# Two halves for the last output tile of a sliding-window attention and token-mixing kernel, with all instruction orders solved anew

## The chip, the cores and the metric

The kernel runs on one core of a Trainium2 chip. The metric is the device time of one execution in microseconds; the median of three runs is 137.68 us (136.97 to 139.27). The engines are PE (matrix products and transposes), ACT (activations and copies), DVE (elementwise work and copies), POOL (here mostly the issuing of loads and some stores) and SP (which only issues stores and two first loads).

## What is computed

The inputs are q, k and v of 8 batches, 8 heads, 576 positions and 64 elements per head, and three weights. For each batch and head there is attention over a causal window of 128 positions with a linear bias by distance; the heads are put side by side to a row x of 512, and a token mixer follows:

```
scores = q @ k.T / 8 - slope[h] * |distance|     where 0 <= distance < 128
attn   = exp(scores - max) / sum
x      = concat over heads of attn @ v           # 576 x 512 per batch
W      = (x @ w_q) @ (x @ w_k).T / 8             # 576 x 576 per batch
out    = relu(W @ x) @ w_out                     # 576 x 512 per batch, float32
```

The kernel uses that W @ x is (x @ w_q) @ ((x @ w_k).T @ x), so that W is never made.

## The kernel before, in words

The kernel is a list of some 775 operations with names, each put on one engine. A text, ORDER, names them one by one with their engine (P, A, V, G for POOL, S for SP), the PSUM bank of a matmul operation, and a number of filling matmuls ahead of it. The loop at line 885 walks this text and emits each operation; every engine then works through its own in that order, one after the other, and waits where the data of its next operation is not ready. The order comes from a planner outside the kernel, which uses the costs written beside each operation (for instance `pe(0.865, 0.2)`). In the names, the first number is the batch.

- L (Lq, Lk, Lv, Lt, Lw..): loads, all issued by POOL, except FQ0 and FQ1, the two halves of the first q tile, which SP issues and CQ0, CQ1 turn into 16 bits. `load` (line 366) lets each load wait for an earlier one, so that only a few are in flight.
- TW, TN, TT: transposes of q and k on PE, and ETW, ETN, ETT their evictions. QK: scores of a group of blocks. EXP: the exponential of 128 x 1024 scores on ACT (line 610), 64 in all. MUL: the product with the bias (line 617, DVE). PV: the product with v. X: normalization (lines 655 and 656, DVE).
- XT, WQ, WK, G, MX with their evictions EXT, EWQ, EWK, EG, RM: the token mixer of a batch.
- OUT (`add_out`, line 800): an output tile of 128 positions by 512 columns, four matmuls that are summed in one bank; EO: its eviction into a free buffer on ACT or DVE; DO: its store from SP or POOL. Tiles whose number ends in 4 hold the last 64 positions of two batches, and take two DMAs.
- At the start stand constants: iota (POOL), idh, perm, dist and mask (DVE), bias0 and bias1 (ACT), and memsets (ones0 to ones4, zeros, zerop, pads), which can be put on DVE or POOL.
- HOLD: from its place in the order on, the next store of SP also waits for one of the last loads (`gate`, lines 224 to 227).

The last tile, OUT7.3, is special: its one bank is evicted in two halves of 256 columns (HO7.3.0 on ACT, HO7.3.1 on DVE) into the buffer osb_end, with two stores (DO7.3.0 on SP, DO7.3.1 on POOL). Both evictions name the whole operation OUT7.3 as what they wait for.

`apart` (line 243) tells the scheduler which instructions need not wait for each other: those on different engines that use different halves of a pair of PSUM banks, and those of one named group, which write different columns of one buffer.

Of the kernel before, what the change touches and what calls it, by code (L numbers as in the profile page):

```python
# [45 lines left out]
QK0.3.1:P:0:1 ETW1.1.1:A PV0.0:P:3 Lv0.4:G MUL0.2.1:V EXP0.3.1:A PV0.1:P:2 X0.0:V Lk2.1:G  # L46
QK1.0.1:P:1 QK1.1.1:P:0 EXP1.0.1:A Lq2.1:G X0.1:V PV0.2:P:3 EXP1.1.1:A MUL0.3.1:V XT0.0:P:2
QK0.3.0:P:1 Lk2.0:G X0.2:V EXP0.3.0:A QK1.3.1:P:0 MUL1.0.1:V QK1.2.1:P:3 Lq2.0:G EXP1.2.1:A
TW1.0:P:1 MUL0.3.0:V MUL1.1.1:V Lv1.0:G EXT0.0:A PV0.3:P:3 ETW1.0.0:V ETW1.0.1:A Lwk:G
PV0.4:P:2 EXP1.3.1:A X0.3:V Lv1.1:G QK1.1.0:P:1 wqq:V EXP1.1.0:A QK1.0.0:P:3 QK1.2.0:P:0  # L50
Lv1.2:G X0.4:V EXP1.0.0:A XT0.1:P:1 Lv1.3:G MUL1.3.1:V TW2.1:P:2 EXP1.2.0:A MUL1.2.1:V
Lv1.4:G WQ0.0:P:30 EXT0.1:V ETW2.1.0:A Lt1.0:G XT0.2:P:31 QK1.3.0:P:0 ETW2.1.1:A EWQ0.0:V
WQ0.1:P:10 MUL1.1.0:V EXT0.2:A EXP1.3.0:A QK2.0.1:P:2 Lwo.3:G MUL1.0.0:V WQ0.2:P:11
TW2.0:P:3 EXP2.0.1:A EWQ0.1:V Lwo.2:G MUL1.3.0:V Lk3.0:G PV1.0:P:0 ETW2.0.1:A MUL1.2.0:V
WK0:P:10 ETW2.0.0:A X1.0:V Lt1.1:G PV1.1:P:2 EWQ0.2:A EWK0:A QK2.0.0:P:3 X1.1:V Lwo.1:G
PV1.2:P:1 EXP2.0.0:A QK2.2.1:P:0 Lq3.0:G X1.2:V PV1.3:P:2 EXP2.2.1:A PV1.4:P:3 Lt1.3:G
X1.3:V XT1.0:P:1 QK2.1.0:P:0 Lt1.2:G EXT1.0:A X1.4:V G0:P:20 EXP2.1.0:A Lwo.0:G XT1.1:P:1
Lv2.3:G EG0:V XT1.2:P:21 WQ1.0:P:30 EXT1.1:A MUL2.0.1:V EXT1.2:A MX0.0:P:0 EWQ1.0:A Lk3.1:G
MX0.1:P:1 MX0.2:P:2 RM0.2:V WQ1.2:P:31 WK1:P:30 RM0.1:A Lq3.1:G RM0.3:V RM0.4:A WQ1.1:P:01
EWK1:A Lv2.0:G RM0.0:V QK2.1.1:P:2 EWQ1.1:A QK2.2.0:P:1 EXP2.1.1:A MUL2.1.0:V G1:P:30  # L60
Lv2.2:G EWQ1.2:V TW3.0:P:0 EXP2.2.0:A EG1:V MUL2.1.1:V Lq4.1:G MX1.1:P:2 ETW3.0.0:A TT1:P:3
ETW3.0.1:V MX1.0:P:1 Lv2.1:G RM1.3:A OUT0.2:P:00 RM1.1:V RM1.2:A Lv2.4:G MUL2.2.1:V RM1.0:A
OUT1.3:P:01 ETT2:A ETT3:V Lk4.0:G EO0.2:A MUL2.2.0:V QK2.3.0:P:1 QK2.3.1:P:2 EO1.3:V Lk4.3:G
EXP2.3.0:A QK3.0.0:P:3 OUT1.2:P:00 MUL2.0.0:V EXP2.3.1:A Lq5.2:G MUL2.3.0:V TW3.1:P:1
EO1.2:V Lv3.1:G EXP3.0.0:A PV2.0:P:2 MUL2.3.1:V OUT0.0:P:01 Lk4.1:G ETW3.1.1:A X2.0:V
ETW3.1.0:A PV2.3:P:3 Lk4.2:G EO0.0:A QK3.0.1:P:1 X2.3:V PV2.1:P:2 Lq4.0:G EXP3.0.1:A
QK3.1.0:P:0 QK3.1.1:P:3 X2.1:V Lv3.0:G EXP3.1.0:A OUT1.1:P:10 MUL3.0.0:V Lt2.3:G EXP3.1.1:A
PV2.2:P:2 MUL3.1.0:V PV2.4:P:0 Lq4.3:G EO1.1:A X2.2:V QK3.3.1:P:3 Lq4.2:G OUT0.1:P:11
EXP3.3.1:A X2.4:V Lv3.2:G XT2.1:P:2 MUL3.1.1:V MX1.2:P:3 EO0.1:A QK3.2.0:P:0 OUT0.3:P:10
Lt2.2:G RM1.4:A EXT2.1:V EXP3.2.0:A MUL3.0.1:V Lv3.3:G XT2.2:P:11 XT2.0:P:3 QK3.3.0:P:2  # L70
EXT2.2:A EO0.3:V TN4.1.0:P:0 Lk5.1:G EXP3.3.0:A OUT1.4:P:11 ETN4.1.0:V Lv4.0:G MUL3.2.0:V
EXT2.0:A QK3.2.1:P:0 TN4.1.1:P:2 MUL3.3.1:V EXP3.2.1:A TN4.0.0:P:3 Lt2.0:G OUT1.0:P:10
ETN4.1.1:V Lt2.1:G ETN4.0.0:A MUL3.3.0:V TN4.0.1:P:0 EO1.4:A Lk5.0:G QK4.0.1:P:2 ETN4.0.1:V
PV3.0:P:3 EXP4.0.1:A WQ2.0:P:11 MUL3.2.1:V Lq5.1:G PV3.1:P:0 EWQ2.0:A X3.0:V QK4.1.1:P:2
EO1.0:A Lv3.4:G WK2:P:11 EXP4.1.1:A X3.1:V Lq5.0:G WQ2.1:P:10 EWK2:A QK4.1.0:P:3 MUL4.0.1:V
XT3.0:P:2 Lq5.3:G EXP4.1.0:A QK4.0.0:P:0 EXT3.0:V G2:P:11 Lv4.1:G EWQ2.1:V EXP4.0.0:A
PV3.2:P:2 MUL4.1.0:V Lk5.2:G QK4.2.1:P:3 EG2:A X3.2:V PV3.3:P:0 EXP4.2.1:A Lv4.2:G TT2:P:1
X3.3:V MX2.1:P:2 ETT5:A MX2.0:P:3 Lk6.2:G RM2.1:A WQ3.0:P:11 RM2.3:V ETT4:A PV3.4:P:0
EWQ3.0:A Lk5.3:G RM2.0:V RM2.2:A QK4.2.0:P:2 TN5.1.0:P:1 X3.4:V EXP4.2.0:A OUT2.3:P:30
Lv4.4:G MUL4.0.0:V Lv4.3:G ETN5.1.0:A QK4.3.0:P:0 TN5.0.1:P:2 MUL4.1.1:V EO2.3:A TN5.0.0:P:1  # L80
# [853 lines left out]
```

## Time and profile before

| | |
|---|---|
| median of three runs | 137.68 us (136.97 to 139.27) |
| the profiled execution | 136.75 us |
| its span, first to last instruction | 134.9 us |
| granted TensorE clock, mean | 0.990 |
| first exponential starts | 9.70 us |
| last exponential starts | 110.89 us |
| last matmul ends | 129.78 us |
| last store is issued, and lands | 130.94 us, 2.0 us later |

All times in the profile count from the start of the span. A row of the timeline gives the start, the duration, the engine, the line of the kernel, the operation, what it writes and reads with its shape, how many instructions are merged in the row and, in brackets, how long the engine sat idle before it and what ended that wait. Rows of neighbours overlap a little, since the end of one instruction and the start of the next are pipelined. A row of a group gives the busy sum, the mean in ns and the idle time ahead of it. Most matmuls have the line of the helper `mm` (L216), transposes L219, evictions L231 to L239, loads L222 and stores L225.

### The profile page before, as it was taken

Reading aid. Unit: us, or ns where it says so; the run is one execution under the profiler, and the core shown is the slowest. Engines: PE = TensorE matmul, PEld = TensorE weight load, DVE = VectorE, ACT = ScalarE, POOL = GpSimd, SP = SyncE. Lnnn points to the kernel's source line nnn. Section 1 sums busy time; section 2 is a strip of 40 time slices with the busy share of each in tenths; the row PEclk is TensorE's granted clock in tenths of the full one; section 3 lists DMA queues with packets and bytes.
Section 4 is the critical chain, followed back from the end, with each engine's and each line's share of the span. In section 5 each row is a group of like instructions: output and inputs, shape, how many; then the busy total and the mean of one; then the engine's idle time right before and its main releaser. Section 6 shows DMA issues by size and latency. Waiting matters only on the chain.

```text
span 134.9 us, 5631 instructions
## 1 busy us (share of the span) xinstructions
PE 124.2 (92%) x2390; PEld 82.8 (61%) x2390; DVE 112.4 (83%) x252; ACT 115.6 (86%) x191; POOL 100.0 (74%) x149
## 2 busy tenths in 40 slices
...
GB/s 117 153 183 172 168 179 195 183 152 163 165 178 173 156 155 156 154 154 145 148 150 139 144 149 140 145 140 150 313 217 256 381 305 84 311 174 237 301 313 69
DMA packets 92855, 24.86 MB, mean 184 GB/s; under 512 B 80256, under 2 KB 89344, under 8 KB 92832
## 3 DMA queue, kind: packets, MB, share of 16 engines
...
q14 instruction: 5, 0.04, 0.1%
...
## 4 chain that ended last, share of the span: by engine, by line
POOL 52%; DMA 19%; PE 15%; issue 10%; POOLq 0%; ACT 0%
POOL natw L222 24%; POOL vt L222 16%; PE pair L216 14%; DMA natw<-in_k_dram 11%; DMA vt<-in_v_dram 8%; POOL natt L222 6%; POOL out_dram L225 4%; POOL wout_sb L222 2%; PE pair L219 1%; ACT natw L231 0%; POOLq L929 0%; POOL wk_sb L222 0%; POOL wint L289 0%; POOLq L222 0%; ACT wqT L231 0%
## 5 line engine op out<-in xcount | busy, mean ns | idle before, releaser
L610 ACT ACTIVATE pt<-pair 128x1024 f16<-128x1024 f32 x64 | 63.5, 1038 | 2.7 <-PE pair L216 1.7
L222 POOL DMA_DIRECT2D vt<-in_v_dram x40 | 37.9, 1019 | 2.2 <-DMA vt<-in_v_dram 0.8
L617 DVE TENSOR_TENSOR pt<-pt,bias 128x1024 f16<-128x1024 f16 x48 | 32.1, 682 | 0.1
L216 PE MATMUL pair<-wout_sb,rm 128*128 128x512 f16 x128 | 32.0, 380 | 0.0
L225 POOL DMA_DIRECT2D out_dram<-natw x17 | 10.4, 709 | 19.2 <-ACT natw L231 19.2
L222 POOL DMA_DIRECT2D natw<-in_k_dram x24 | 23.0, 1000 | 1.6 <-DMA natw<-in_q_dram 1.4
L216 PEld LDWEIGHTS <-pt 128*128 128x128 f16 x576 | 20.5, 97 | 5.8 <-issue 3.2
L216 PE MATMUL pair<-qkT 64*128 64x256 f16 (+3 forms) x352 | 22.9, 243 | 1.2 <-ACT pt L610 0.5
L216 PE MATMUL pair<-vt,pt 128*128 128x65 f16 x576 | 23.4, 193 | 0.6 <-DMA vt<-in_v_dram 0.4
L656 DVE TENSOR_TENSOR x<-pair,inv 128x512 f16<-128x512 f32 x32 | 22.1, 692 | 1.1
L222 POOL DMA_DIRECT2D natw<-in_q_dram x23 | 21.9, 1017 | 0.6 <-DMA natw<-in_k_dram 0.4
L216 PEld LDWEIGHTS <-rm 128*128 128x128 f16 x128 | 10.6, 97 | 11.2 <-issue 1.3
L216 PEld LDWEIGHTS <-qkT 64*128 64x128 f16 x352 | 11.2, 94 | 7.5 <-issue 3.7
L219 PEld LDWEIGHTS <-natw 128*64 128x64 f16 (+1 forms) x512 | 12.8, 102 | 4.6 <-issue 2.4
L231 ACT COPY natw<-pair 128x512 f32<-128x512 f32 x21 | 12.7, 612 | 1.7 <-PE pair L216 1.7
L756 ACT ACTIVATE rm<-pair 128x512 f16<-128x512 f32 x20 | 11.3, 613 | 1.6 <-PE pair L216 1.5
L617 DVE TENSOR_TENSOR pt<-pt,biasl 128x1024 f16<-128x1024 f16 x16 | 10.9, 683 | 0.2 <-ACT pt L610 0.2
L219 PE MATMUL pair<-permh,natw 128*64 128x128 f16 x256 | 8.8, 220 | 1.5 <-ACT pt L610 1.2
L655 DVE RECIPROCAL inv<-pair 128x8 f32<-128x8 f32 (+1 forms) x40 | 8.1, 203 | 2.2 <-PE pair L216 2.0
L216 PE MATMUL pair<-xT,wqq_sb 128*128 128x256 f16 x64 | 9.5, 274 | 0.0
L216 PE MATMUL pair<-fill 128*128 128x512 f16 x22 | 7.7, 504 | 1.6 <-DVE fill L347 1.2
L498 ACT COPY qkT<-pair 128x512 f32<-128x512 f32 x12 | 7.0, 625 | 1.5 <-PE pair L219 1.5
...
## 6 DMA issues: line engine op xcount, KB each, us to landing
vt<-in_v_dram POOLq DMA_DIRECT2D x32, 128.0 KB, 5.9
...
natw<-in_q_dram POOLq DMA_DIRECT2D x16, 128.0 KB, 5.2
natw<-in_k_dram POOLq DMA_DIRECT2D x16, 128.0 KB, 5.1
...
```

What stands on the lines that cost most here:

```text
L216: hold(nc.tensor.matmul(*a, **k))
L219: hold(nc.tensor.transpose(*a))
L222: hold(nc.gpsimd.dma_start(**k))
L225: i = (nc.gpsimd if eng == "POOL" else nc.sync).dma_start(**k)
L231: hold(nc.scalar.copy(out_ap, in_ap))
L498: hold(nc.scalar.copy(dst, src))
L610: nc.scalar.activation(out=pt[:, 0:1024], in_=two(s.bank).rearrange("p e c -> p (e c)"), func=AF.Exp, scale=SCALE)
L617: nc.vector.tensor_tensor(out=pt[:, 0:1024], in0=pt[:, 0:1024], in1=bt, op=ALU.mult)
L655: nc.vector.reciprocal(out=inv[r], in_=pxv[r, :, :, 64])
L656: nc.vector.tensor_tensor(out=x[r].rearrange("p (g h d) -> p g h d", g=2, h=4), in0=pxv[r, :, :, 0:64], in1=inv[r].unsqueeze(3).broadcast_ ...
L756: hold(nc.scalar.activation(out=out_ap, in_=in_ap, func=AF.Relu, scale=WSCALE))
```

## The change

The last tile becomes two operations, OUT7.3.1 and OUT7.3.0, of four matmuls on 256 columns each, in two PSUM banks of different pairs. Each has its own eviction and store; the two evictions are put in a group (`last`), since they write different columns of osb_end. HO7.3.1 goes to ACT and its store to SP; HO7.3.0 goes to DVE and its store to POOL.

The whole ORDER is solved anew by the planner, so nearly every operation changes its place, and some their engine or bank: the set of names is the same but for OUT7.3. Filling matmuls are 31 in place of 22, zerop goes from POOL to DVE and zeros from DVE to POOL, stores are shared differently by SP and POOL, and HOLD stands at the end, behind all stores. The diff, with those lines of ORDER that start and end it or bear on the stores:

```diff
 ORDER = """
-FQ1:S ones0:V FQ0:S iota:G Lk0.0:G ones3:V ones1:V Lk0.1:G idh:V zeros:V Lq0.1:G CQ1:A
-dist:V Lk1.1:G CQ0:A mask:V Lt0.3:G Lt0.1:G perm:V bias0:A pads:V Lq1.1:G TW0.0.0:P:00:13
-Lt0.2:G ones4:V TW0.0.1:P:01 ETW0.0.0:V Lt0.0:G ETW0.0.1:A zerop:G bias1:A QK0.2.0:P:1:3
-QK0.1.0:P:2 Lv0.0:G EXP0.1.0:A TW0.1:P:0:5 Lv0.1:G EXP0.2.0:A QK0.0.0:P:3 ETW0.1.1:A
-ETW0.1.0:V Lv0.2:G EXP0.0.0:A biasl1:V QK0.2.1:P:0 QK0.1.1:P:1 MUL0.2.0:V QK0.0.1:P:2
-Lq1.0:G EXP0.1.1:A biasl0:V Lk1.0:G EXP0.0.1:A MUL0.0.0:V TW1.1:P:1 ones2:G MUL0.1.1:V
-EXP0.2.1:A MUL0.0.1:V TT0:P:2 Lv0.3:G ETW1.1.0:A ETT0:V MUL0.1.0:V Lwq:G ETT1:A
...
-OUT4.0:P:11 EXP6.3.0:A PV6.0:P:0 DO1.1:G OUT4.3:P:10 X6.0:V EXP6.1.1:A Lv7.4:G TN7.0.0:P:3
...
-EXP6.3.1:A X5.4:V OUT4.1:P:30 DO3.2:G MUL6.1.1:V ETN7.1.0:A XT5.2:P:31 QK6.1.0:P:0 XT5.1:P:2
...
-PV6.4:P:0 Lv7.3:G MUL6.2.0:V WQ5.2:P:30 DO3.3:S WQ5.1:P:31 ETN7.1.1:A PV6.1:P:2 X6.4:V
...
-EXT6.0:A G5:P:20 DO1.0:S EXP7.2.1:A MUL7.0.0:V HOLD:S DO4.1:S MX4.2:P:3 XT6.1:P:0 EG5:V
...
-EWQ6.1:V QK7.3.1:P:0 EWK6:A MUL7.1.1:V MX5.1:P:3 EXP7.3.0:A G6:P:21 MUL7.0.1:V OUT5.1:P:20
-RM5.1:A MUL7.3.0:V EXP7.3.1:A MUL7.2.1:V OUT5.0:P:10 RM5.3:A EG6:V PV7.1:P:0 MUL7.3.1:V
-EO5.1:A OUT5.3:P:11 EO5.0:A DO5.1:S X7.1:V DO5.0:G MX6.0:P:3 MUL7.2.0:V MX6.1:P:2 EO5.3:A
-DO2.0:G PV7.4:P:0 RM6.3:A DO5.3:S PV7.3:P:1 RM6.0:A X7.4:V OUT5.2:P:21 DO4.2:S RM6.2:A
-X7.3:V RM6.1:A PV7.0:P:0 PV7.2:P:3 EO5.2:A X7.0:V OUT6.3:P:20 X7.2:V OUT6.1:P:10 EO6.3:A
-MX5.2:P:0 XT7.2:P:11 DO6.3:G XT7.0:P:3 EO6.1:V EXT7.2:A XT7.1:P:2 EXT7.0:A OUT6.0:P:11
-DO4.0:G EXT7.1:V RM5.4:A DO6.1:G WQ6.2:P:10 WK7:P:00 EWQ6.2:A EO6.0:A WQ7.2:P:30 WQ7.1:P:01
-EWQ7.2:V EWK7:A DO6.0:G WQ7.0:P:31 EWQ7.1:A G7:P:30 DO3.4:G EWQ7.0:A MX6.2:P:2 OUT5.4:P:10
-EG7:A RM6.4:V DO2.3:G MX7.0:P:0 DO5.2:G MX7.1:P:3 EO5.4:V MX7.2:P:2 OUT6.2:P:11 RM7.1:A
-RM7.4:V DO5.4:S RM7.2:V RM7.0:A OUT7.4:P:10 RM7.3:A EO6.2:V OUT7.1:P:00 DO6.2:S EO7.4:A
-OUT7.2:P:01 DO7.4:S EO7.1:V OUT7.0:P:20 DO7.1:G EO7.2:A OUT7.3:P:21 DO7.2:S EO7.0:A DO7.0:S
-HO7.3.0:A HO7.3.1:V DO7.3.0:S DO7.3.1:G
+FQ0:S ones3:V FQ1:S Lk0.0:G zerop:V iota:G ones2:V Lk0.1:G pads:V Lq0.1:G dist:V Lt0.2:G
+CQ1:A idh:V mask:V Lq1.1:G zeros:G perm:V bias1:A Lk1.1:G TW0.0.1:P:00:13 CQ0:A Lt0.0:G
+bias0:A ETW0.0.1:V TW0.0.0:P:01:1 Lt0.3:G ones0:V ones4:G ones1:V ETW0.0.0:A biasl0:V
+QK0.1.0:P:1:5 Lv0.0:G QK0.0.0:P:2 biasl1:V EXP0.1.0:A QK0.2.0:P:3 Lt0.1:G TW0.1:P:0:1
+EXP0.0.0:A Lv0.1:G ETW0.1.1:V ETW0.1.0:A Lv0.2:G EXP0.2.0:A MUL0.0.0:V QK0.1.1:P:1:4
+QK0.2.1:P:2 MUL0.1.0:V Lk1.0:G QK0.0.1:P:0 EXP0.2.1:A MUL0.2.0:V Lq1.0:G TW1.1:P:3:2
+EXP0.0.1:A MUL0.2.1:V Lv0.3:G EXP0.1.1:A MUL0.0.1:V Lv0.4:G ETW1.1.0:V ETW1.1.1:A TT0:P:0:4
+Lq2.0:G MUL0.1.1:V PV0.0:P:2 ETT1:A QK1.0.1:P:1 ETT0:V Lk2.0:G X0.0:V EXP1.0.1:A QK0.3.0:P:0
...
+EO1.4:A Lt2.1:G ETN4.0.0:V XT2.1:P:3 EXP3.2.0:A OUT1.0:P:01 DO1.2:G MUL3.3.0:V EXT2.1:A
...
+OUT2.0:P:11 Lv5.2:G EXP5.0.0:A MUL5.0.1:V XT4.1:P:0 Lq6.3:G QK5.2.1:P:3 EO2.0:A MUL5.0.0:V
+QK5.2.0:P:2 EXP5.2.1:A OUT3.1:P:10 DO2.0:S EXT4.1:V Lt3.3:G MUL5.1.1:V EXP5.2.0:A
...
+OUT4.0:P:11 EXP6.1.1:A X6.0:V PV5.4:P:0 EO4.1:V EO4.0:A QK6.3.1:P:2 TN7.1.1:P:3 X5.4:V
+EXP6.3.1:A DO4.0:S OUT4.2:P:11 DO2.2:S MUL6.1.1:V ETN7.1.1:A XT5.2:P:10 TN7.0.0:P:0 DO3.4:S
+TN7.1.0:P:2 EO4.2:V EXT5.2:A QK6.3.0:P:3 ETN7.1.0:A OUT3.3:P:10 MUL6.2.0:V DO4.2:G
+EXP6.3.0:A DO0.3:S MUL6.3.1:V WQ5.0:P:11 DO4.1:G DO0.1:S ETN7.0.0:A EO3.3:V TN7.0.1:P:2
+DO3.1:G XT5.1:P:3 EWQ5.0:A ETN7.0.1:V QK6.2.1:P:0 EXT5.1:A PV6.1:P:1 Lv7.1:G MUL6.3.0:V
+EXP6.2.1:A WQ4.2:P:20 QK7.1.0:P:3 X6.1:V DO3.0:G WK5:P:21 EWQ4.2:A EXP7.1.0:A PV6.4:P:0
+DO1.4:G MUL6.2.1:V WQ5.2:P:20 EWK5:A QK7.1.1:P:1 X6.4:V EWQ5.2:A PV6.2:P:3 EXP7.1.1:A
+DO2.3:G QK7.0.1:P:2 X6.2:V PV6.3:P:0 DO1.1:G EXP7.0.1:A WQ5.1:P:10 MUL7.1.0:V Lv7.4:G
+XT6.0:P:3 EWQ5.1:A QK7.0.0:P:2 X6.3:V Lv7.0:G EXT6.0:A XT6.2:P:11 G5:P:10 EXP7.0.0:A
+EXT6.2:V MX4.2:P:3 Lv7.2:G XT6.1:P:0 EG5:V WQ6.0:P:11 RM4.4:A EXT6.1:V MX5.0:P:2 MUL7.0.1:V
+QK7.3.1:P:3 MX5.1:P:0 RM5.0:A WK6:P:10 MUL7.1.1:V RM5.2:A WQ6.1:P:20 EWQ6.0:V EXP7.3.1:A
+EWK6:V OUT5.0:P:21 RM5.3:V RM5.1:A MUL7.3.1:V QK7.3.0:P:1 EWQ6.1:A QK7.2.0:P:3 EXP7.3.0:A
+QK7.2.1:P:0 EO5.0:V G6:P:20 MUL7.0.0:V EXP7.2.1:A OUT5.3:P:21 EG6:V MUL7.3.0:V EXP7.2.0:A
+MX6.0:P:1 MX6.1:P:0 MUL7.2.1:V OUT5.1:P:20 EO5.3:A RM6.0:V RM6.2:A DO5.3:G PV7.4:P:3
+MUL7.2.0:V RM6.3:A PV7.0:P:1 DO2.1:G OUT6.0:P:21 RM6.1:A X7.4:V EO5.1:A DO5.0:G PV7.1:P:0
+X7.0:V EO6.0:A PV7.3:P:3 DO0.0:G X7.1:V OUT6.3:P:20 DO6.0:S DO1.3:S X7.3:V PV7.2:P:1 EO6.3:A
+DO3.3:S WQ6.2:P:21 OUT5.2:P:00 X7.2:V DO6.3:G XT7.2:P:01 XT7.0:P:3 EWQ6.2:V DO0.2:G EO5.2:A
+EXT7.2:V XT7.1:P:1 MX5.2:P:2 OUT6.1:P:01 EXT7.0:A EXT7.1:V DO4.3:G RM5.4:V WK7:P:00 EO6.1:A
+WQ7.2:P:30 WQ7.0:P:31 EWK7:V DO6.1:S WQ7.1:P:10 EWQ7.0:V DO5.2:S MX6.2:P:2 EWQ7.1:A G7:P:00
+RM6.4:A DO5.1:S OUT5.4:P:11 EG7:A DO3.2:S EWQ7.2:A MX7.2:P:0 DO1.0:S MX7.0:P:2 MX7.1:P:3
+EO5.4:A RM7.4:V OUT6.2:P:10 RM7.2:V RM7.0:A DO5.4:G RM7.1:A RM7.3:V OUT7.4:P:00 EO6.2:A
+OUT7.0:P:01 DO6.2:G EO7.4:A OUT7.1:P:11 DO7.4:S EO7.0:A OUT7.2:P:20 EO7.1:V DO7.0:S
+OUT7.3.1:P:21 DO7.1:S EO7.2:A OUT7.3.0:P:30 HO7.3.1:A DO7.2:S HO7.3.0:V DO7.3.1:S DO7.3.0:G
+HOLD:S
 """
@@ -806,24 +807,28 @@
 
         need = [*wto]
         need += [erm[b, 2 * r + st // 2] for r in range(2)] if st < 4 else [erm[b, 4], erm[b - 1, 4]]
+        if (b, st) == (NB - 1, 3):
+
+            for h in range(2):
+                def emh(o, h=h):
+                    for db in range(4):
+                        mm(one(o.bank)[:, 0:256], rm_s[b % 2][1][:, db, P:2 * P],
+                           wout_sb[:, db, 256 * h:256 * h + 256], start=(db == 0), stop=(db == 3))
+
+                t = osd[b, st] = add(f"OUT{b}.{st}.{h}", pe(0.44, 0.2), need, emh, banks=1)
+                def ev2(o, t=t, h=h):
+                    cp(o.eng, osb_end[:, 256 * h:256 * h + 256], one(t.bank)[:, 0:256])
+
+                e = add(f"HO{b}.{st}.{h}", EV(0.26, 0.34), [t], ev2, frees=[t], group="last")
+
+                def dm2(o, h=h):
+                    store(o.eng, out=out[b, P * st:P * st + P, 256 * h:256 * h + 256], in_=osb_end[:, 256 * h:256 * h + 256])
+
+                add(f"DO{b}.{st}.{h}", {"SP": (0.6, 0.6), "POOL": (0.7, 0.7)}, [e], dm2, serve=0.36)
+            return
         t = add(f"OUT{b}.{st}", pe(0.865, 0.2), need, em, banks=1)
         osd[b, st] = t
         box = {}
-
-        if (b, st) == (NB - 1, 3):
-
-            for h in range(2):
-                cols = slice(256 * h, 256 * h + 256)
-
-                def ev2(o, cols=cols):
-                    cp(o.eng, osb_end[:, cols], one(t.bank)[:, cols])
-
-                def dm2(o, cols=cols):
-                    store(o.eng, out=out[b, P * st:P * st + P, cols], in_=osb_end[:, cols])
-
-                e = add(f"HO{b}.{st}.{h}", EV(0.26, 0.34), [t], ev2, frees=[t])
-                add(f"DO{b}.{st}.{h}", {"SP": (0.6, 0.6), "POOL": (0.7, 0.7)}, [e], dm2, serve=0.36)
-            return
 
         def ev(o):
             box["o"] = osb_s[o.ring]
```

111 lines of the change are left out of this document (50 added, 61 removed).

## The prediction, made before the change was run

> **What bounds the kernel now.** I read the page first, then the table by stage, then the timeline of the two ends.
>
> ```profile
> span 134.9 us, 5631 instructions
> ...
> PE 124.2 (92%) x2390; PEld 82.8 (61%) x2390; DVE 112.4 (83%) x252; ACT 115.6 (86%) x191; POOL 100.0 (74%) x149
> ```
> The span is 134.9 us; the execution that was profiled took 136.75 us, so 1.85 us lie around the span. The median of the three timed runs, 137.68 us, is 0.9 us above that execution, and these three lie 2.3 us apart: 2% (2.75 us) is about what a measurement of this kernel can tell from no change. No engine has much room: PE, ACT and DVE are all above 80%.
>
> ```profile
> 60.00:65.00 5.00, 5.00 (x114) 3.67 (x111) 4.90 (x12) 4.97 (x8) 5.00 (x7) 1.00 2.28 147
> ...
> 85.00:90.00 5.00, 5.00 (x99) 3.23 (x96) 4.81 (x12) 4.19 (x10) 5.00 (x8) 1.00 2.24 143
> ...
> 105.00:110.00 5.00, 5.00 (x114) 3.74 (x110) 4.96 (x12) 5.00 (x9) 0.00 (x0) 1.00 1.04 386
> 110.00:115.00 5.00, 5.00 (x75) 2.96 (x70) 4.47 (x10) 4.70 (x9) 1.14 (x2) 1.00 0.31 114
> ...
> 125.00:130.00 5.00, 4.78 (x23) 1.96 (x20) 1.90 (x4) 3.05 (x7) 0.54 (x1) 1.00 0.90 288
> ```
> Columns: the stretch, its length, busy time of PE, PEld, DVE, ACT, POOL, then the granted clock, the DMA share and GB/s. In the middle (60 to 65 us) four engines are full at once. From 110 us on ACT and DVE thin out and PE alone carries the end (4.78 of 5 us). So a microsecond saved or lost counts at the start (everything behind it is full), in the middle if a queue stops, and in the PE-bound end.
>
> **The change part by part: the halves.** The last tile, as it is now:
>
> ```profile
> 119.37 1.04 PE L216 MATMUL pair<-wout_sb,rm 128*128 128x512 f16 x4
> ...
> 121.06 1.04 PE L216 MATMUL pair<-xT,wqq_sb 128*128 128x256 f16 x8
> ...
> 126.16 3.62 PE L216 MATMUL pair<-wout_sb,rm 128*128 128x512 f16 x16
> ...
> 128.95 0.58 ACT L231 COPY osb<-pair 128x512 f32<-128x512 f32 x1 [0.28 <-PE pair L216]
> 129.82 0.37 ACT L231 COPY osb_end<-pair 128x256 f32<-128x256 f32 x1 [0.28 <-PE pair L216]
> 130.21 0.33 SPq L225 DMA_DIRECT2D out_dram<-osb_end  x1
> 130.22 0.42 DVE L233 COPY osb_end<-pair 128x256 f32<-128x256 f32 x1 [2.23 <-ACT osb_end L231]
> 130.94 0.54 POOL L225 DMA_DIRECT2D out_dram<-osb_end  x1 [2.12 <-DVE osb_end L233]
> ```
> PE ends at 126.16 + 3.62 = 129.78. ACT copies one half (129.82 to 130.19), and only then does DVE copy the other: it sat idle for 2.23 us and was released by ACT, not by PE. The last store is issued at 130.94 behind it. The two copies read one bank; the change gives each half its own bank and puts the copies in a group of their own, so the wait of DVE on ACT goes. What is late next is PE: the second half is complete when PE ends, and DVE can begin at 129.82 in place of 130.22. That is **-0.40 us**. ACT's half leaves the path: with EO7.2 on ACT until about 129.5 its copy ends near 129.9 and SP's store follows, ahead of the other.
>
> The price is eight matmuls of 256 columns, with eight weight loads, in place of four of 512. The rows cost both: eight of 256 took 1.04 us, four of 512 took 1.04 us. I take 0; the bounds are 0 and +0.2. The Trainium skill, "TensorE: Matmul & The Clock Gate", section "Back-to-back issue gap", speaks against the split: in a stream of weight load and matmul the spacing is set by both, and it gives 81 ns at N=128 and 131 ns at N=512 as sustained. Taken between these (98 ns at N=256, an estimate from that page) the halves would cost 8 x 98 - 4 x 131 = 260 ns more, and -0.40 would become -0.14. Here the rows give the same time for both, so the page's figures are not what this kernel shows, and the rows decide.
>
> **The start.** Each column's order is one in-order queue, so I walked the first words of each queue with the rows of before.
>
> ```profile
> 1.24 0.28 DVE L322 MEMSET vt<- 64x264 uint32 x1
> 1.61 0.21 DVE L324 MEMSET vt<- 128x8 f16 x5
> 1.92 0.28 DVE L322 MEMSET vt<- 64x264 uint32 x1
> ...
> 2.97 0.24 DVE L281 TENSOR_SCALAR identh<-wint 128x128 f16<-128x128 int32 x1
> ...
> 3.68 0.23 DVE L297 TENSOR_SCALAR farb<-wint 128x256 int32<-128x256 int32 x1
> 3.70 1.27 ACT L231 CAST natw<-osb 128x512 f16<-128x512 f32 x2 [1.69 <-DMA osb<-in_q_dram]
> ...
> 4.27 0.42 DVE L293 TENSOR_TENSOR far<-far 128x256 f32<-128x256 f32 x1
> 4.73 0.42 DVE L294 TENSOR_TENSOR wm<-far,wint 128x256 f32<-128x256 f32 x1
> ...
> 5.19 1.34 ACT L304 ACTIVATE bias<-wm 128x256 f16<-128x256 f32 x4 [0.21 <-DVE wm L294]
> 5.29 0.55 DVE L339 MEMSET xtl<- 128x256 uint32 x2
> ...
> 6.21 0.28 DVE L322 MEMSET vt<- 64x264 uint32 x1
> ...
> 7.98 0.58 ACT L498 COPY qkT<-pair 128x512 f32<-128x512 f32 x1 [1.46 <-PE pair L219]
> ...
> 8.63 0.63 PE L216 MATMUL pair<-qkT 64*128 64x256 f16 x8
> 8.67 0.96 POOL L335 MEMSET pt<- 128x64 f16 x10
> ...
> 9.19 1.25 PE L216 MATMUL pair<-fill 128*128 128x512 f16 x5
> ...
> 9.70 1.92 ACT L610 ACTIVATE pt<-pair 128x1024 f16<-128x1024 f32 x2
> 10.38 1.08 PE L219 MATMUL pair<-permh,natw 128*64 128x128 f16 x32
> ...
> 11.98 2.88 ACT L610 ACTIVATE pt<-pair 128x1024 f16<-128x1024 f32 x3
> ```
> Now wm is ready at 5.15, and the first exponentials run from 9.70. In the new order DVE does ones3, zerop, ones2, pads, dist, idh, mask. One set of ones is 0.68 us (1.24 to 1.92), pads 0.92 (5.29 to 6.21), dist 0.59 (3.68 to 4.27), idh 0.24, mask 0.88 (4.27 to 5.15). zerop moves from POOL to DVE, where no row shows it: ten memsets are at least 0.42 (twice the five of 0.21) and at most POOL's 0.96; I take 0.6, nearer to DVE's own row. From 1.24: 0.68 + 0.6 + 0.68 + 0.92 + 0.59 + 0.24 + 0.88 = 4.59, so wm is ready at 5.8, 0.7 us later. ACT's queue now has bias1 between the two casts: bias1 5.9 to 7.2, CQ0 0.6 to 7.8, bias0 1.3 to 9.1, ETW0.0.0 0.6 to 9.7; then QK0.1.0 (0.63) and the first exponential at about 10.2, 0.5 us late. TW0.1 stands behind three QK instead of two: PE reaches it at 9.7 + 3 x 0.6 = 11.5 and ends at 12.6. ACT has two exponentials ahead of ETW0.1.0, done at 12.1, waits, evicts until 13.1, and starts the third one there, where before it started at 11.98. The slip is **1.1 us**; by zerop's bounds 0.9 to 1.5. The fills (31 in place of 22) stand where PE waits for evictions or loads in this reckoning, and cost nothing; if that cover is gone, the four fills ahead of QK0.1.1 are 1.0 us (five took 1.25).
>
> How much of the slip arrives at the end?
>
> ```profile
> 18.47 3.77 ACT L610 ACTIVATE pt<-pair 128x1024 f16<-128x1024 f32 x4 [0.53 <-PE pair L216]
> ...
> 33.89 0.58 ACT L237 COPY xT<-pair 128x512 f32<-128x512 f32 x1 [0.43 <-PE pair L219]
> ```
> ACT idles for 0.53 and 0.43 us in these places before everything fills up. If a late stream finds its matmuls ready there, 0.96 us comes back; if PE is as late as ACT, nothing. I take half: **+0.6 us** stays, bounds 0 and +1.5.
>
> **The middle.** The tiles' work is the same; only meeting points move. ACT and DVE trade evictions almost evenly (by the words, among others: ACT gets four EO and two EG more and loses two ETW, one ETN, three ETT and two EWK). I take 0. What could not be hidden is priced as rivals.
>
> **Queues.** POOL takes DO1.2 among the loads, behind the 32nd exponential of 64 and so near 61 us, where POOL is full; that is 0.7 us of it, which the loads behind it bear, and PE waits for no load there now, so I take 0. Later POOL takes DO4.2, DO4.1, DO3.1, DO3.0, DO1.4 (two DMAs), DO2.3 and DO1.1 ahead of its last loads.
>
> ```profile
> 97.79 1.82 POOL L222 DMA_DIRECT2D vt<-in_v_dram  x2
> 113.72 1.14 POOL L225 DMA_DIRECT2D out_dram<-natw  x2 [14.11 <-ACT natw L231]
> ```
> ```profile
> L225 POOL DMA_DIRECT2D out_dram<-natw x17 | 10.4, 709 | 19.2 <-ACT natw L231 19.2
> ...
> vt<-in_v_dram POOLq DMA_DIRECT2D x32, 128.0 KB, 5.9
> ```
> ```profile
> 110.89 1.07 ACT L610 ACTIVATE pt<-pair 128x1024 f16<-128x1024 f32 x1
> ```
> POOL's loads now end at 99.6 and it then idles for 14.1 us. In the new order DO4.2 waits for an eviction whose word stands behind the 54th exponential of 64; the first starts at 9.70 and the last at 110.89, 1.6 us apart, which puts it near 97 us; eight issues at 0.71 and four V loads at 0.91 are 9.3 us, so the last load goes out at about 106 and lands 5.9 us later, at 112. Its users, PV7.3 and PV7.2, are the last two PV of all. I take 0, with a bound of +1. SP loses its gate (HOLD comes last), so DO2.0 can go out as soon as EO2.0 is done, beside the loads; all other SP stores queue behind DO4.0, which waits for EO4.0 behind the 53rd exponential, so nothing else comes early. I take 0, bound +0.5.
>
> **The end.** Behind the last exponential PE had 13 output tiles; in the new order it has 12 (one more is done earlier). A tile is 0.87 us. PE is full at 105 to 110 too, so the tile may just push other work: bounds -0.87 and 0, I take 0, nearer to that row.
>
> **Sum.** -0.40 + 0.6 + 0 = +0.2 us on 136.75, that is 136.95; against the median it is **137.9 us**. With the bounds: -0.40 - 0.87 + 0 = -1.3 and -0.2 + 1.5 + 1 + 0.5 = +2.8 (136.4 to 140.5 against the median).
>
> **Rivals.** *ACT's queue stops in the middle* (ends slower). Evictions stand ahead of exponentials in one in-order queue; where an eviction's matmuls are late, all later exponentials are. A single such stop is the 0.43 or 0.53 us quoted. With the start's +0.2 it takes six such stops more than now (6 x 0.48 = 2.9) to pass 2%: +3.1, **140.8 us**. For it: four engines are full at 60 us, so a stop is nowhere made up. Against it: the work and its balance are the same. *The middle packs better*: ACT has 0.81 us idle at 85 to 90 and 0.30 at 110 to 115; with those two filled, the slip swallowed, the tile earned and the halves earned it is -1.1 - 0.87 - 0.40 = -2.4, **135.3 us**, half of it below 134.9 if other stretches of ACT give something too. Against it: the start as walked above is later. *Stores bunch*: by the words 5.6 MB of stores stand behind the last exponential in place of 4.9 MB; the extra 0.77 MB at 288 GB/s are 2.7 us if all of them delay the last store, and half, +1.3, is likelier, as 110 to 115 us moved only 114 GB/s: **139.2 us**. The Trainium skill, "DMA: Bandwidth & Descriptors", section "Queues, rings and completion order", says that a completion lands only after every earlier write of that DMA engine, across its queues, which would make the last store wait for these; no row here can show it. *The halves do nothing* (DVE still waits for ACT): +0.6, **138.3 us**.
>
> **How the numbers follow.** Forecast 0.44 (own range 136.6 to 139.2), ACT's queue stops 0.28, packs better 0.18, stores bunch 0.06, halves do nothing 0.04. Faster by over 2% (below 134.9) is half of "packs better" and the forecast's far edge: 0.11. Slower by over 2% (above 140.4) is most of the first rival and half of the stores: 0.28. Within 2%: 0.61. The range goes from 135.2 to 141.0: it reaches past the first rival's 140.8 and past the third's, and leaves out the outer half of the two outer cases, about 0.2.
>
> **What would show it.** DVE's copy to osb_end released by PE and within 0.1 us of PE's end; the first exponential at 10.2 and the third at 13.1; the loads ending near 107 and no PE wait on vt; the last store landing within 2.1 us. Idle ACT in the middle above that of before, released by PE, would prove the first rival. It is wrong if the third exponential is on time, or if the distance from the start to the last exponential changes by more than 1.5 us.

## The result, and the profile after

The changed kernel takes 138.03 us (median of 22 runs, 137.38 to 138.72) where the kernel before, run beside it, takes 137.25 us (22 runs, 136.29 to 139.27). The ratio is 1.0062, with a 95% interval of 1.0042 to 1.0082: **slower by about 0.85 us**, small but resolved, and inside the 2% that the prediction called no change. The execution that was profiled took 137.93 us against 136.75 before, with a span of 136.2 us against 134.9. Of the profiles shown further down, those of runs 1 and 8 are of executions that were slower as a whole, and of these two only distances within their start and their tail are used.

The first lines of the page of the changed kernel, and its table by stage (columns: the stretch, its length, busy time of PE, PEld, DVE, ACT and POOL, granted clock, DMA share, GB/s):

```profile
span 136.2 us, 5660 instructions
...
PE 126.3 (93%) x2403; PEld 84.2 (62%) x2403; DVE 114.4 (84%) x262; ACT 115.3 (85%) x189; POOL 100.4 (74%) x142
```
```profile
60.00:65.00 5.00, 4.87 (x109) 3.71 (x106) 4.27 (x11) 4.83 (x9) 5.00 (x7) 1.00 2.11 137
...
105.00:110.00 5.00, 5.00 (x119) 3.96 (x115) 4.78 (x11) 4.46 (x9) 2.53 (x4) 1.00 1.34 255
110.00:115.00 5.00, 5.00 (x56) 2.54 (x54) 5.00 (x10) 5.00 (x8) 0.00 (x0) 1.00 0.65 45
125.00:130.00 5.00, 5.00 (x35) 2.40 (x34) 2.31 (x4) 3.33 (x6) 1.64 (x3) 1.00 0.87 289
```
PE is busy for 4.87 to 5.00 of the 5 us in each of these stretches, and for 2.1 us more in all than before (126.3 against 124.2). The same table cut in other places, first before, then after:

```profile
0.00:20.00 20.00, 16.23 (x246) 9.30 (x247) 14.11 (x57) 15.35 (x25) 16.63 (x40) 1.00 1.45 162
20.00:40.00 20.00, 18.30 (x444) 14.60 (x445) 18.59 (x39) 18.86 (x31) 18.03 (x25) 1.00 1.69 172
40.00:120.00 80.00, 79.86 (x1617) 53.67 (x1612) 75.48 (x150) 75.46 (x124) 61.26 (x78) 1.00 1.85 182
```
```profile
10.00:20.00 10.00, 9.54 (x186) 6.11 (x181) 8.53 (x18) 9.51 (x12) 8.87 (x12) 1.00 1.92 174
0.00:20.00 20.00, 17.18 (x239) 9.57 (x240) 15.67 (x64) 14.96 (x24) 17.34 (x33) 1.00 1.47 160
20.00:40.00 20.00, 18.41 (x442) 14.83 (x439) 17.81 (x38) 18.66 (x31) 17.43 (x24) 1.00 1.72 179
40.00:120.00 80.00, 79.82 (x1611) 53.52 (x1607) 75.81 (x152) 74.74 (x122) 62.59 (x81) 1.00 1.83 170
```
Up to 20 us PE is busy for 0.95 us more than before (17.18 against 16.23), from 20 to 40 us for 0.11 us more, from 40 to 120 us for the same, and what is left of the 2.1 us lies behind 120 us, as PE ends 1.15 us later. From 40 to 120 us PE is full to within 0.2 us in both kernels, so what PE lacks at 40 us should arrive at the end, but for the last few microseconds. Busy time alone does not show this, since a busy PE need not do the same work at the same pace; run 11 below bears it out. Two places are left: the start, where PE is now 95% busy between 10 and 20 us (in part with filling matmuls, which do no work), and the end.

The end of the changed kernel in the timeline (start, duration, engine, line, operation; lines of helpers are one higher than before):

```profile
128.16 2.76 PE L217 MATMUL pair<-wout_sb,rm 128*128 128x512 f16 x16
...
130.57 0.38 ACT L232 COPY osb_end<-pair 128x256 f32<-128x256 f32 x1
131.03 0.42 DVE L234 COPY osb_end<-pair 128x256 f32<-128x256 f32 x1 [1.11 <-ACT osb_end L232]
131.13 0.64 SPq L226 DMA_DIRECT2D out_dram<-osb_end  x1
131.76 0.55 POOL L226 DMA_DIRECT2D out_dram<-osb_end  x1 [3.67 <-DVE osb_end L234]
```
PE ends at 128.16 + 2.76, that is at 130.93 (rows are rounded), and DVE starts its half 0.10 us later, where it started 0.44 us after PE before. The profile still puts DVE's wait down to ACT's copy, but that copy now ends at 130.95, as PE does, and no longer 0.41 us behind PE. The last store is issued 0.83 us after PE's end in place of 1.16. But the time from issue to landing of the two last stores grew; the first fence is of before, the second of after:

```profile
DMA to landing us min/median/max: 2.0/2.1/2.1
```
```profile
DMA to landing us min/median/max: 2.5/2.6/2.8
```
From PE's end to the end of the span it is 5.17 us before and 5.23 after (from the unrounded times of the traces; the page gives the span to 0.1 us). The 0.33 us that the halves gain at the issue is not there at the end of the span.

### The profile page after: what moved, and what is told of

Same layout as the page of the kernel before. It is cut to its first block, busy times and chain, and to the rows that moved or that the text cites. A ratio compares the mean times of both kernels' runs of the same rounds, so it can differ in the third digit from the quotient of the medians.

```text
span 136.2 us, 5660 instructions
## 1 busy us (share of the span) xinstructions
PE 126.3 (93%) x2403; PEld 84.2 (62%) x2403; DVE 114.4 (84%) x262; ACT 115.3 (85%) x189; POOL 100.4 (74%) x142
## 4 chain that ended last, share of the span: by engine, by line
PE 73%; ACT 10%; issue 6%; DMA 4%; DVE 2%; POOL 1%; POOLq 0%
PE pair L217 63%; PE pair L220 11%; ACT pt L611 7%; DMA natw<-in_k_dram 4%; ACT xT L238 1%; POOL out_dram L226 1%; ACT qkT L499 1%; DVE xtl L657 1%; DVE x L657 1%; DVE pt L618 1%; ACT natw L232 0%; POOLq L934 0%; DVE inv L656 0%; POOLq L226 0%; POOLq L923 0%
## 5 line engine op out<-in xcount | busy, mean ns | idle before, releaser
L223 POOL DMA_DIRECT2D vt<-in_v_dram x40 | 36.9, 955 | 1.6 <-issue 1.1
L217 PE MATMUL pair<-wout_sb,rm 128*128 128x512 f16 (+1 forms) x132 | 32.4, 374 | 0.0
L223 POOL DMA_DIRECT2D natw<-in_k_dram x24 | 22.2, 963 | 2.6 <-DMA vt<-in_v_dram 1.2
L217 PE MATMUL pair<-qkT 64*128 64x256 f16 (+3 forms) x352 | 23.4, 243 | 0.2 <-DVE qkT L240 0.2
L232 ACT COPY natw<-pair 128x512 f32<-128x512 f32 x25 | 14.9, 610 | 3.7 <-PE pair L217 2.9
L757 ACT ACTIVATE rm<-pair 128x512 f16<-128x512 f32 x19 | 10.7, 611 | 0.6 <-PE pair L217 0.5
L217 PE MATMUL pair<-fill 128*128 128x512 f16 x31 | 9.6, 439 | 1.4 <-DVE fill L348 1.2
L217 PE MATMUL pair<-xT,wqq_sb 128*128 128x256 f16 x64 | 9.0, 274 | 0.0
L759 DVE TENSOR_SCALAR rm<-pair 128x512 f16<-128x512 f32 x13 | 8.7, 682 | 0.0
```

The lines of the kernel that those rows point to most:

```text
L217: hold(nc.tensor.matmul(*a, **k))
L223: hold(nc.gpsimd.dma_start(**k))
L232: hold(nc.scalar.copy(out_ap, in_ap))
L757: hold(nc.scalar.activation(out=out_ap, in_=in_ap, func=AF.Relu, scale=WSCALE))
L759: hold(nc.vector.tensor_scalar(out=out_ap, in0=in_ap, scalar1=0.0, scalar2=WSCALE, op0=ALU.max, op1=ALU.mult))
```

## The experiments

Each ratio is against the kernel before, timed beside it; one per mille is 0.14 us. "Old order" is the order of before with the last tile as two operations, unless something else is said.

**1 and 2. The two parts of the change, one at a time.** Run 1 keeps the order of before and splits the last tile; run 2 takes the new order and leaves the last tile whole.

```diff
 run 1, old order:
-OUT7.3:P:21 ... HO7.3.0:A HO7.3.1:V DO7.3.0:S DO7.3.1:G
+OUT7.3.0:P:21 OUT7.3.1:P:30 ... HO7.3.0:A HO7.3.1:V DO7.3.0:S DO7.3.1:G
 run 2, new order:
-OUT7.3.1:P:21 ... OUT7.3.0:P:30 HO7.3.1:A ... HO7.3.0:V DO7.3.1:S DO7.3.0:G
+OUT7.3:P:21 ... HO7.3.1:A ... HO7.3.0:V DO7.3.1:S DO7.3.0:G
```


> The order of before, with only the last tile split: OUT7.3.0 and OUT7.3.1 one behind the other in the place of OUT7.3, in two banks, the copies on ACT and DVE as before. Theory (the halves are worth what the trace of the change shows from PE's end to the last store's issue, 0.83 us in place of 1.16): 0.3 us faster than before, about 136.95, ratio 0.998; DVE's copy starts within 0.1 us of PE's end. Rival (DVE still waits for ACT, or the extra matmuls cost what the wait gave): no gain, ratio 1.000 or above.

> The order of the change with the split undone: one OUT7.3 in one bank, two copies of it. Theory (the new order costs, the halves give a little back): 0.3 us slower than the changed kernel, ratio to before 1.008 or 1.009. Rival (the halves themselves cost, by eight weight loads and a second group of copies): faster than the changed kernel, ratio below 1.005.

Measured: run 1, 0.9983 (0.9947 to 1.0019); run 2, 1.0073 (1.0034 to 1.0111). The loss belongs to the new order, and the halves are worth -0.2 us with an uncertainty of 0.5 in the old order and -0.15 us, with 0.6, in the new one (1.0062 against 1.0073, not timed beside each other). The tails, run 1 first:

```profile
131.31 0.42 DVE L233 COPY osb_end<-pair 128x256 f32<-128x256 f32 x1 [1.84 <-PE pair L216]
131.48 0.42 SPq L225 DMA_DIRECT2D out_dram<-osb_end  x1
132.03 0.54 POOL L225 DMA_DIRECT2D out_dram<-osb_end  x1 [1.73 <-DVE osb_end L233]
```
```profile
128.23 2.75 PE L216 MATMUL pair<-wout_sb,rm 128*128 128x512 f16 x12
...
131.41 0.33 SPq L225 DMA_DIRECT2D out_dram<-osb_end  x1
131.42 0.42 DVE L233 COPY osb_end<-pair 128x256 f32<-128x256 f32 x1 [1.44 <-ACT osb_end L231]
132.15 0.55 POOL L225 DMA_DIRECT2D out_dram<-osb_end  x1 [3.99 <-DVE osb_end L233]
```
With the halves DVE is released by PE (run 1); with one bank it is released by ACT (run 2), 0.44 us after PE's end at 130.98. And twelve matmuls of 512 columns take 2.75 us in run 2, where the changed kernel does eight of 512 and eight of 256 in 2.76: splitting the columns costs PE nothing here.

**3 and 4. Start and end of the two orders exchanged at the 57th exponential.**

```diff
 run 3: the words of before to the 58th exponential, then those of the new order
 run 4: the words of the new order to the 57th exponential, then those of before
```


> The order of before up to the 58th of 64 exponentials, then all remaining operations in the order of the change, with the halves. Theory (the new order loses 0.4 us at the start and some 0.9 us in the end from 102 us on, and the middle comes out even): the start is that of before, so 0.4 us better than the change: ratio 1.002 to 1.006. Rival (the middle loses, the end is better): ratio 0.992 to 0.997.

> The order of the change up to the 57th of 64 exponentials, then all remaining operations in the order of before, with the halves. Theory (start loses 0.4 us, middle even, end as before and 0.3 us for the halves): ratio 0.999 to 1.002, faster than the change. Rival (the middle loses): ratio 1.006 or above, as the change or slower.

Measured: 1.0478 (1.0426 to 1.053) and 1.0491 (1.043 to 1.0552), both far from every expectation. At these places the two orders had done different sets of operations, and the ones left over stand together at the joint. In run 3:

```profile
106.30 1.02 ACT L610 ACTIVATE pt<-pair 128x1024 f16<-128x1024 f32 x1 [1.06 <-PE pair L216]
```
The next exponential starts at 113.14, 6.8 us later; in the changed kernel no two neighbours at the end are more than 2.8 us apart. These two runs say nothing of the change, only what such a joint costs: 5%.

**5 and 6. The same at the 49th exponential**, where the sets of finished operations agree.

```diff
 run 5: the words of the new order to the 49th exponential, then those of before (with the halves)
 run 6: the words of before to the 49th exponential, then those of the new order
```


> The order of the change up to the 49th exponential, the order of before from there, with the halves. At this joint both orders have done the same set of PE, ACT and DVE operations, apart from memsets, so that the joint itself should cost nothing, unlike the joints at the 57th and 58th. Theory (PE bounds everything from about 18 us on; by PE work left at each exponential the new order loses 0.4 us at the start, 0.7 us between the 21st and the 33rd exponential, nothing from there to the 57th, and 0.3 us net from the 57th to the end): about 1 us slower than the order of before, ratio 1.004 to 1.009. Rival (the loss is all in the end, behind the 57th): ratio 0.996 to 1.001.

> The order of before up to the 49th exponential, the order of the change from there, with the halves; the sets at the joint differ by two small operations. Theory (as for the run with the parts the other way round): only the end's 0.3 us and the longer landing of the last store remain: ratio 1.000 to 1.004, better than the change. Rival (the loss is all in the end): ratio 1.005 to 1.009, as the change.

Measured: run 5, 1.0094 (1.0063 to 1.0124), just above its range of 1.004 to 1.009; run 6, 1.004 (1.0007 to 1.0072), at the upper edge of its range. Beside run 1's 0.9983 the larger loss is in the first part of the new order, but run 6 is not free of one. In its profiled execution 0.69 us of it lie behind the last matmul (5.86 us to the end of the span, where before has 5.17), and PE too ends 0.78 us later than before (130.56), with a stop of 0.62 us ahead of 31.15 that is taken up under run 11.

**7 and 8. Do late stores hold up the last one?** Eight stores of old tiles are put earlier in the new order, five in the old one.

```diff
 run 7, new order:
+ DO2.1:G DO0.0:G DO0.2:G DO4.3:G   ahead of DO5.3:G
+ DO1.3:S DO3.3:S DO3.2:S DO1.0:S   ahead of DO6.0:S
 run 8, old order:
+ DO4.2:S                           ahead of DO5.1:S
+ DO2.0:G DO4.0:G DO3.4:G DO2.3:G   ahead of DO5.0:G
```


> The changed kernel with eight stores whose data are long ready moved forward in their queues (DO1.3, DO3.3, DO3.2, DO1.0 on SP ahead of DO6.0; DO2.1, DO0.0, DO0.2, DO4.3 on POOL ahead of DO5.3); nothing else is changed. Theory (stores bunch at the end: the last store lands 2.5 us after its issue because the writes ahead of it still drain): PE's end stays, the last store lands in 2.0 to 2.1 us, 0.4 us less than the change: ratio 1.003. Rival (the landing does not hang on the stores ahead): landing 2.5 or more, ratio 1.006.

> The order of before with the halves (as the first experiment) and five long-ready stores moved forward (DO4.2 on SP ahead of DO5.1; DO2.0, DO4.0, DO3.4, DO2.3 on POOL ahead of DO5.0). Theory: from PE's end to the end of the span 4.7 us in place of the 5.12 us of before and of the first experiment, where the 0.4 us that the halves gave at the issue went into a longer landing: ratio 0.996 or 0.997, the best so far. Rival (landing does not hang on the stores ahead): 5.1 us, ratio 0.998 to 1.000.

Measured: run 7, 1.0036 (1.0003 to 1.0069), the ratio as expected, but not told apart from the changed kernel's 1.0062; run 8, 1.0046 (1.0013 to 1.0079), where 0.996 to 0.997 was expected: a miss. In run 7 the landing of the last two stores went from 2.5 to 2.8 us only to 2.4 to 2.7, and in run 8 it was 3.0. That earlier stores queue ahead of the last one is not supported.

**9 and 10. Exchanged at the 11th exponential (near 22 us).**

```diff
 run 9: the first 94 words of the new order, then those of before (with the halves)
 run 10: the first 102 words of before, then those of the new order
```


> The new order's first 94 words (up to the 11th exponential, near 22 us), then the order of before with the halves; at this joint the two orders have done the same operations but for one QK and one EXT. Nothing is left out. The old order with halves alone gave 0.9983, the new order to the 49th exponential and the old one behind it 1.0094. Theory (the loss is made at the start, the prediction's term of +0.6 with its fills): 1.004 to 1.010. Rival (the loss is made between the 11th and the 49th exponential): 0.996 to 1.001.

> The mirror image: the old order's first 102 words (up to the 11th exponential), then the new order; at this joint two products with the bias differ. Nothing is left out. Theory (loss at the start): 0.997 to 1.001. Rival (loss between the 11th and the 49th exponential): 1.004 to 1.010, as the whole new order has 1.0062.

Measured: run 9, 1.0085 (1.0048 to 1.0123), in the theory's range: the new order's first 22 us with the old order behind them cost as much as the whole new order. Run 10, 1.0294 (1.0248 to 1.0341), fits neither. But PE stops behind both joints, for a load of q, first in run 9, then in run 10:

```profile
26.70 1.08 PE L219 MATMUL pair<-permh,natw 128*64 128x128 f16 x32 [0.90 <-DMA natw<-in_q_dram]
```
```profile
27.19 1.92 PE L220 MATMUL pair<-permh,natw 128*64 128x128 f16 x32 [2.49 <-DMA natw<-in_q_dram]
```
In neither kernel does PE wait for a load of q there; that the two orders load in a different sequence is the likely reason. The 2.49 us make run 10 useless for the question. The 0.90 us in run 9's profile are 0.7% by themselves, so its ratio can come from the joint, and run 9 does not show by itself that the start is to blame.

**11. The new order with 12 of its 31 filling matmuls taken out.**

```diff
-TW0.1:P:0:1   QK0.1.1:P:1:4   TW1.1:P:3:2   TT0:P:0:4   PV0.2:P:3:1
+TW0.1:P:0     QK0.1.1:P:1     TW1.1:P:3     TT0:P:0     PV0.2:P:3
```


> The changed kernel without its 12 filling matmuls behind the first transposes of the second half of the heads (4, 2, 4, 1 and 1); 19 fills are left. No result changes, as fills write nothing that is read. The prediction's step (fills stand where PE waits anyway, and cost nothing): 1.005 to 1.008, as the changed kernel. Rival (their cover is gone, and PE is behind for good): the fills take 12 x 0.22 = 2.6 us of PE and 0.5 to 1 us of it comes back, 0.998 to 1.002. Third possibility (PE's granted clock falls for want of them): above 1.010, with a mean clock below 0.98.

Measured: **0.9989 (0.9957 to 1.0021)**, in the rival's range. Against the changed kernel, which was not timed beside it, that is 0.9989 / 1.0062 = 0.9927, or 1.0 us, with an interval of 0.989 to 0.997 (0.5 to 1.5 us) when the two uncertainties are put together. The granted clock is 0.991 in the mean of the 12 executions (0.977 to 1.0) and 0.996 in the mean of the changed kernel's 22 (0.989 to 1.0). Three of the 12 lie at 0.977 to 0.983, below all of the 22, and take 137.4 to 138.0 us. So the clock may have fallen a little for want of fills, but not to the third possibility's mean below 0.98, and the kernel is faster all the same.

What the fills did is seen in the timeline at two places, each time first of the changed kernel, then of this run. One is QK0.1.1, whose twelve matmuls stand for it and the two QK behind it:

```profile
11.78 1.04 PE L217 MATMUL pair<-fill 128*128 128x512 f16 x4
...
12.75 0.85 PE L217 MATMUL pair<-qkT 64*128 64x256 f16 x12
```
```profile
12.42 0.85 PE L217 MATMUL pair<-qkT 64*128 64x256 f16 x12 [1.05 <-ACT qkT L499]
```
Without fills PE waits here for 1.05 us, for an eviction, until 12.42. With the four fills, and one ahead of TW0.1, it goes on at 12.75. Of these 0.33 us 0.15 were there from the first exponential on (10.10 against 9.95), and 0.18 is what the fills run beyond the wait. The other place is TT0:

```profile
15.41 1.02 PE L217 MATMUL pair<-fill 128*128 128x512 f16 x4 [0.25 <-ACT pt L611]
...
16.37 0.41 PE L220 MATMUL pair<-identh,natt 64*128 64x64 f16 x16
...
17.51 1.94 ACT L611 ACTIVATE pt<-pair 128x1024 f16<-128x1024 f32 x2 [0.32 <-PE pair L217]
```
```profile
15.18 0.29 PE L220 MATMUL pair<-identh,natt 64*128 64x64 f16 x8 [0.75 <-ACT pt L611]
...
16.08 0.29 PE L220 MATMUL pair<-identh,natt 64*128 64x64 f16 x8 [0.61 <-DMA natt<-in_k_dram]
...
17.11 1.94 ACT L611 ACTIVATE pt<-pair 128x1024 f16<-128x1024 f32 x2 [0.31 <-PE pair L217]
```
Without fills the transposes of TT0 begin at 15.18, and their second half waits for a load until 16.08. With four fills ahead, all of TT0 begins at 16.37. It ends at 16.78 in place of 16.37, and the seventh exponential starts 0.40 us later (17.51 against 17.11): 0.15 from the first exponential on, 0.13 more by the sixth, and 0.12 here. So nearly all of the 1.02 us of these four fills is hidden under the two waits of run 11. In the other executions with this start (runs 2, 4, 7 and 9) the seventh exponential is 0.24 to 0.29 us behind run 11's, and the first one within 0.04: some 0.25 us for the fills of both places together. In run 5 that load came later still (the second half of TT0 ran at 17.05), so the fills ahead of TT0 were covered whole, and the load held the exponential up.

A second step of the distance between these two executions comes at 30 us; first the changed kernel, then run 11:

```profile
30.83 0.30 PE L217 MATMUL pair<-vt,pt 128*128 128x65 f16 x4 [0.56 <-issue]
...
31.51 1.02 ACT L611 ACTIVATE pt<-pair 128x1024 f16<-128x1024 f32 x1 [0.54 <-PE pair L217]
```
```profile
29.57 0.42 PE L217 MATMUL pair<-vt,pt 128*128 128x65 f16 x8
...
30.42 1.99 ACT L611 ACTIVATE pt<-pair 128x1024 f16<-128x1024 f32 x2
```
A product with v stops half-way for 0.56 us, and the 17th exponential is 1.09 us behind run 11's. From there to the last exponential the distance stays between 1.05 and 1.13 us, and PE ends at 129.89 in run 11, 1.04 us earlier. This second stop is also in run 2, smaller in run 4, and not in runs 5, 7 and 11. But it does not follow the fills: of the executions that keep the old order from the start to this place, and so lack the twelve, before and run 3 don't have it, and runs 1, 6, 8 and 12 do, for 0.59 to 1.05 us. Run 12:

```profile
30.94 0.63 PE L216 MATMUL pair<-vt,pt 128*128 128x65 f16 x15 [0.59 <-issue]
```
And run 7, with all 31 fills and without the stop, is only 0.2 us behind run 11 at the last exponential (112.36 against 112.16). So the profiles show some 0.25 us of what the fills cost; that it is 1.0 us (0.5 to 1.5) rests on the times of the many runs, and where the rest is lost stays open. The profile names no releaser for the stop ("issue"). That it is a load of v, late because loads wait for each other, is argued, not shown.

**12. The two last stores exchange their queues**, in the old order with the halves.

```diff
-HO7.3.0:A HO7.3.1:V DO7.3.0:S DO7.3.1:G
+HO7.3.0:A HO7.3.1:V DO7.3.0:G DO7.3.1:S
```


> The old order with halves (0.9983; stores of the halves issued 0.55 us apart, landing 2.3 to 2.4), with the queues of the two half stores exchanged: the first on POOL, the last on SP. In all runs POOL's issue starts 0.3 us behind the eviction that it waits for, SP's within 0.05. Theory A (that 0.3 us is on the path): the last store is issued 0.5 us behind PE's end in place of 0.75, with a landing as before, so 0.996 to 0.998. Theory B (the closer the two last stores, the longer the landing): the two are less than 0.2 us apart, the landing grows to 2.8 or more, and the ratio is 0.998 to 1.002. From the last matmul to the span's end: A 4.8, B 5.1 or more.

Measured: 0.9964 (0.9927 to 1.0001), the best of all runs, but its interval still touches 1. In its tail

```profile
130.23 0.42 DVE L233 COPY osb_end<-pair 128x256 f32<-128x256 f32 x1 [1.84 <-PE pair L216]
130.51 0.54 POOL L225 DMA_DIRECT2D out_dram<-osb_end  x1 [1.28 <-ACT osb_end L231]
130.69 0.33 SPq L225 DMA_DIRECT2D out_dram<-osb_end  x1
```
POOL starts its issue 0.29 us after ACT's copy (129.84 + 0.38 = 130.22), SP 0.04 us after DVE's (130.65). The last issue comes 0.49 us after PE's end at 130.20 (0.75 in run 1), and the span ends 5.00 us after PE (5.12 in run 1). Half of the gain at the issue reached the end: the ratio is at the lower edge of theory A's, the tail between the two theories.

The tails of all runs but 3, 4 and 10 (us; the time from PE's end to the last issue, the distance between the two last issues, the landing, and the time from PE's end to the end of the span, unrounded as above):

| run | last tile | PE end to issue | between issues | landing | PE end to span end |
|---|---|---|---|---|---|
| before | whole | 1.16 | 0.73 | 2.0 to 2.1 | 5.17 |
| 2 | whole | 1.17 | 0.74 | 2.1 to 2.2 | 5.17 |
| after | halves | 0.83 | 0.63 | 2.5 to 2.8 | 5.23 |
| 1 | halves | 0.75 | 0.55 | 2.3 to 2.4 | 5.12 |
| 5 | halves | 1.14 | 0.39 | 2.7 to 2.8 | 5.33 |
| 6 | halves | 0.85 | 0.02 | 2.8 to 3.1 | 5.86 |
| 7 | halves | 0.83 | 0.63 | 2.4 to 2.7 | 5.15 |
| 8 | halves | 0.75 | 0.17 | 3.0 | 5.77 |
| 9 | halves | 0.75 | 0.51 | 2.7 to 2.9 | 5.44 |
| 11 | halves | 0.83 | 0.64 | 2.4 to 2.5 | 5.12 |
| 12 | halves, queues exchanged | 0.49 | 0.18 | 2.1 to 2.7 | 5.00 |

In the eight kernels with halves and the stores on their old queues the landing is 2.3 us or more, and longest where the two issues are closest. Run 12, with 0.18 us between them and 2.1 to 2.7, does not fit that. What sets the landing stays open.

## Why the prediction was right, and where it was not

The time was forecast at 137.9 us and is 138.03, within 2% of before as forecast. The sum behind it was +0.2 us, and the change is +0.85 us (1.0062 on 137.25). That the time agrees to 0.1 us is luck: the three runs shown beforehand had a median (137.68) 0.43 us above that of the 22 later ones, and the sum's one loss, +0.6 for the start, was not the one that came. Without the twelve fills the same start, middle, end and halves are at 0.9989, -0.15 us in all (-0.6 to +0.3); the loss came with the fills, which the sum put at nothing.

- **The halves, -0.40: right at the issue, -0.33, and not seen at the end.** DVE starts 0.10 us after PE, as forecast, and the 0.41 us that it waited for ACT beyond PE's end are gone. The sign named for it, a release by PE, came in runs 1 and 12 (DVE 0.04 us after PE), but not in the changed kernel, where the profile names ACT; why DVE starts 0.07 us later there is not shown. The step that failed is the one that ended the path at the last issue: the landing was to stay within 2.1 us, and it is 2.5 to 2.8. On the time the halves are -0.2 ± 0.5 us. So the rival in which the halves do nothing is not excluded by the time; its mechanism (DVE held up by ACT as before) did not happen. The 256-column matmuls cost nothing, as the rows said (2.76 against 2.75 us). The Trainium skill, "TensorE: Matmul & The Clock Gate", section "Back-to-back issue gap", would give +0.26 us by the estimate in the prediction; these rows do not show it.
- **The start, +0.6: the place was right, the mechanism was not.** The walk through the queues gave the first exponential 10.2 and the third 13.1 us. Measured are 10.10 and 12.39:

```profile
10.10 1.94 ACT L611 ACTIVATE pt<-pair 128x1024 f16<-128x1024 f32 x2 [0.69 <-PE pair L217]
...
12.39 3.88 ACT L611 ACTIVATE pt<-pair 128x1024 f16<-128x1024 f32 x4
```
The slip at the third is 0.4 us in place of 1.1, and at the eighth exponential it is gone (18.43 against 18.47). wm is ready at 5.83 us, as forecast (5.8), so DVE's part was sized well. Too long was the part on PE. The forecast took 0.6 us for each of three QK ahead of TW0.1, but the row that it read (8.63, 0.63 us) holds eight matmuls, which are two QK of four. All three took 0.85 us, and TW0.1 ended at 11.85 in place of 12.6:

```profile
9.66 0.85 PE L217 MATMUL pair<-qkT 64*128 64x256 f16 x12
...
10.77 1.08 PE L220 MATMUL pair<-permh,natw 128*64 128x128 f16 x32
```
That no +0.6 us of it arrives is seen in run 11, which keeps this start.
- **The fills, 0: this is the step that failed.** The prediction said that they stand where PE waits and cost nothing, and that otherwise the four fills ahead of QK0.1.1 are 1.0 us. Run 11 gives 1.0 us (0.5 to 1.5) for the twelve fills. Those ahead of TW0.1 and QK0.1.1 can be seen to cost 0.13 us at the sixth exponential, and those ahead of TT0 0.12 us more at the seventh, because the waits that covered them were shorter than they are; the rest of the 1.0 us is not located. It was the cover that had to be checked, place by place: what PE waits for there, until when, and how long the fills run.
- **The middle, 0: right.** Run 11, which is the new order and the halves with fewer fills, is at 0.9989, so the middle can hide no large loss. PE is full from 40 to 120 us in both kernels. The rival in which ACT's queue stops needed six more stops than before; ACT's exponentials wait for PE six times in place of four between 20 and 115 us, first before, then after:

```profile
ACT pt L610 <- PE pair L216: 1.1, 4, 0.4
```
```profile
ACT pt L611 <- PE pair L217: 1.7, 6, 0.5
```
PE itself does not go idle at that, so this is no loss.
- **The queues, 0: right.** The last loads are issued until 107.7 us (forecast 106) and loads of v land after 5.4 us in the median:

```profile
105.11 2.63 POOL L223 DMA_DIRECT2D vt<-in_v_dram  x3
```
Between 36 and 120 us PE waits for no load, only twice for 0.2 us on other things. The one product with v that stops, at 30.83, stands far ahead of the moved stores.
- **The end, 0 for one tile less: right.** The last exponential starts 2.3 us later (113.21 against 110.89), and PE ends 17.72 us after it in place of 18.89. It is a trade, since PE is full on both sides of it. The test "wrong if the distance from the start to the last exponential changes by more than 1.5 us" fired on this trade, and so was no good test: the count of exponentials is not the same amount of work in two orders.
- **Stores bunch, +1.3: not seen.** PE's end to span end is +0.06 us, and runs 7 and 8, with the old stores earlier, land no sooner than 2.4 and 3.0 us.

Still open: what sets the landing of the last stores (runs 6, 8 and 12), why run 8 is slower than run 1, and where the part of the fills' 1.0 us beyond the 0.25 us seen is lost. The four kernels with the 31 fills and no bad joint (after and runs 2, 5 and 7) have ratios above 1.003; runs 1, 11 and 12, without the twelve, are at 0.996 to 0.999. Run 6 (1.004) and run 8 (1.0046), which don't have them either, have the two longest tails.
